# A delta-rule chain followed by a Fourier block: keys left unnormalised, weights rounded by integer instructions, and a chunk's outputs moved between the next step's products

## The chip, the core and the metric

One core of a Trainium2 chip runs the whole program. The metric is the device time of one execution in microseconds, from the runs listed below; a profiled execution is one more run of the same program, with its instructions recorded. The engines are TensorE (PE; its weight loads are listed apart as PEld), VectorE (DVE), ScalarE (ACT), GpSimd (POOL) and SyncE (SP, which here only issues transfers). Each takes its instructions strictly in the order in which they were built, and waits on semaphores for the others.

## The reference

There are two blocks. The first is a delta-rule recurrence for 4 batches, 8 heads, 768 steps and head dimension 48. With `k_n = k / (norm(k) + 1e-6)`, each step is

```
y[t]  = q[t] @ state
v_old = k_n[t] @ state
state = state + beta[t] * outer(k_n[t], v[t] - v_old)
```

The outputs, heads side by side (4 x 768 x 384), are the `x` of the second block: `u = x + real(fft(fft(x, axis=1), axis=2))`, then `u + relu(norm(u) @ w_ch1) @ w_ch2`, with `norm` the usual mean and variance over the last axis. `w_ch1` is 384 x 1536 and `w_ch2` 1536 x 384; both arrive as 64-bit floats, and the kernel turns them into 32-bit ones itself.

## The kernel before

The 768 steps of a batch are cut into 12 chunks of 64. Four chunks make a quad (12 quads over the batches), two quads a group (6 groups). For a group, `ahead` runs `prepare` on both quads and then `invert`:

- `prepare` squares the keys (`Ksq`, L302), sums them (L304), takes the root on POOL (`nrm`, L305), adds 1e-6 and inverts (L306, L307), and multiplies the keys by that (L308). TensorE then transposes keys and queries (`pt`, L127), ACT copies them to `KQT`, and the products `pg` of keys with keys and with queries go to `A` (ACT, L350) and `LQ` (DVE, L353).
- `invert` takes beta times the key products, 32 steps to a block, and solves for the inverse by 30 eliminations of two DVE instructions each (L379 and L381), for all blocks of the group at once. It ends with two DVE transposes (`Z`, L388, and L390) and four rounds of small products `pj`, copied by ACT into `wt`.

`chain(m)` then does one chunk: `pk = K state`, `R = V - pk` on DVE (L455), `pu = wt R`, copied by ACT to `U` (L464), `pS = K^T U`, added by DVE to the state (`st`, L475), and the outputs `py` = Q state + LQ U, copied by ACT to `x` (L488). The next chunk needs the new state, so the 48 chunks follow each other.

Beside the chain stand two generators. `pre` is `ahead` of the next group. `side` is, in batch 0, `weights`: 24 parts of 384 columns, in each of which ACT reads the two halves of the 64-bit numbers, POOL takes a maximum (L275), DVE cuts and shifts (L276, L277, L280) and POOL multiplies and adds (L282, L283). In later batches `side` is `second`: the Fourier products (`pf`, `pb`) and the two matrix products of the batch before (`ph` and `po`), with ReLU on ACT (L623). The last loop advances `pre` by 2.4 and `side` by 1.2 to 2.4 steps for each yield of the chain, and all of this is the order in which work is offered to a list scheduler; the scheduler then sets each engine's order with its own idea of durations. What an engine does next can therefore be seen only in the built order.

Sums in PSUM come from four pools: `pair` (2 tiles of two banks: `pg`, `pj`, `pk`, `pS`, `py`), `one` (2 of one bank: `pt`, `pu` and the two small start products) and `post` (2 of one bank, for everything of the second block).

Of the kernel before, what the change touches and what calls it, by code (L numbers as in the profile page):

```python
# [80 lines left out]
def kernel(  # L81
# [159 lines left out]
    def weights():  # L241
# [496 lines left out]
```

## Time and profile before

| | |
|---|---|
| runs | 927.81 us median of 3 (927.21 to 928.8) |
| profiled execution | 929.47 us, span of its instructions 927.8 us |
| mean granted TensorE clock | 0.847 of 2.4 GHz |
| busy: PE, DVE, ACT, POOL | 734.9, 411.7, 278.7, 176.2 us |
| last chunk's `U` (chunk 47) | starts at 772.41 us |
| after that | the second block of batch 3 alone |

How to read the rows further down: `A<-B` says that tile A is written from tile B. `x32` counts instructions. A row of the timeline begins with its start in us and its duration, and ends, in brackets, with the idle time of the engine just before it and what ended that. The granted clock says at which share of 2.4 GHz TensorE ran in a stretch; its other level is 1.2 GHz, 0.5 in the rows.

### The profile page before, as it was taken

Reading aid. Unit: us, or ns where it says so; the run is one execution under the profiler, and the core shown is the slowest. Engines: PE = TensorE matmul, PEld = TensorE weight load, DVE = VectorE, ACT = ScalarE, POOL = GpSimd, SP = SyncE. Lnnn points to the kernel's source line nnn. Section 1 sums busy time; section 2 is a strip of 40 time slices with the busy share of each in tenths; the row PEclk is TensorE's granted clock in tenths of the full one; section 3 lists DMA queues with packets and bytes.
Section 4 is the critical chain, followed back from the end, with each engine's and each line's share of the span. In section 5 each row is a group of like instructions: output and inputs, shape, how many; then the busy total and the mean of one; then the engine's idle time right before and its main releaser. Section 6 shows DMA issues by size and latency. Waiting matters only on the chain.

```text
span 927.8 us, 18288 instructions
## 1 busy us (share of the span) xinstructions
PE 734.9 (79%) x7768; PEld 548.2 (59%) x7768; DVE 411.7 (44%) x970; ACT 278.7 (30%) x649; POOL 176.2 (19%) x160
## 2 busy tenths in 40 slices
PE   1501686225797799988899998999999998999997
PEld 1401565124676667756667776677676766766774
DVE  4478426874468821187631583147821113500000
ACT  0513534235331531323612325243151212211210
POOL 6034634554501210000400004011100001100000
PEclk9755556556577879998799997999989998999999
DMA  7321134303110111210101110010000000000000
GB/s 148 65 82 68 24 97 103 92 1 91 35 18 10 23 23 29 41 42 4 21 17 41 22 43 2 10 27 1 26 11 10 9 10 10 1 17 9 9 18 17
DMA packets 84049, 30.77 MB, mean 33 GB/s; under 512 B 79488, under 2 KB 81216, under 8 KB 83584
## 3 DMA queue, kind: packets, MB, share of 16 engines
q1 hardware_dynamic: 77792, 25.18, 11.8%
q10 hardware_dynamic: 5408, 2.06, 0.9%
q0 software_dynamic: 768, 2.36, 0.7%
q8 instruction: 61, 1.00, 0.4%
q14 instruction: 20, 0.16, 0.1%
HBM read 24.87 MB, written 4.72 MB: 32 GB/s over the span
## 4 chain that ended last, share of the span: by engine, by line
PE 57%; DVE 18%; POOL 10%; ACT 6%; issue 4%; DMA 3%; SPq 2%; POOLq 0%; DVEq 0%; ACTq 0%
PE po L124 19%; PE ph L124 17%; PE py L124 6%; PE pu L124 3%; POOL nrm L305 3%; PE pf L124 3%; DVE X L381 2%; DVE sub L379 2%; PE pt L127 2%; POOL wtmp L275 2%; POOL wtmp L282 2%; PE pg L124 2%; POOL w L283 2%; SPq L153 2%; ACT A L350 1%
## 5 line engine op out<-in xcount | busy, mean ns | idle before, releaser
L124 PE MATMUL ph<-unT,w 128*128 128x256 f32 x864 | 220.5, 402 | 2.0 <-ACT hT L623 0.9
L124 PE MATMUL po<-w,hT 128*128 128x384 f32 x576 | 203.0, 500 | 0.0
L124 PEld LDWEIGHTS ph<-unT,w 128*128 128x128 f32 x864 | 162.7, 197 | 28.5 <-issue 2.5
L124 PEld LDWEIGHTS po<-w,hT 128*128 128x128 f32 x576 | 106.6, 192 | 65.6 <-issue 1.9
L623 ACT ACTIVATE hT<-ph 128x256 f32<-128x256 f32 x144 | 55.3, 384 | 189.3 <-PE ph L124 188.8
L503 POOL DMA_INDIRECT out_dram<-x,rows_hi x12 | 12.6, 1048 | 404.4 <-DVE x L636 246.2
L124 PE MATMUL pj<-Z,A 32*32 32x32 f32 x768 | 18.3, 212 | 79.8 <-DVE Z L388 79.8
L475 DVE TENSOR_TENSOR st<-st,pS 48x192 f32<-48x192 f32 x88 | 30.8, 350 | 89.6 <-PE pS L124 88.4
L381 DVE TENSOR_TENSOR X<-X,sub 128x30 f32<-128x30 f32 (+9 forms) x180 | 67.9, 377 | 4.3
L379 DVE TENSOR_TENSOR sub<-X 128x30 f32<-128x30 f32 (+9 forms) x180 | 66.3, 369 | 4.7
L636 DVE TENSOR_TENSOR x<-x,po 128x384 f32<-128x384 f32 x24 | 13.3, 552 | 118.2 <-PE po L124 118.2
L124 PEld LDWEIGHTS pj<-Z,A 32*32 32x32 f32 x768 | 16.9, 127 | 81.4 <-DVE Z L388 47.6
L455 DVE TENSOR_TENSOR R<-V,pk 128x192 f32<-128x192 f32 x48 | 16.9, 352 | 96.7 <-PE pk L124 96.3
L350 ACT ACTIVATE A<-pg 32x256 f32<-32x256 f32 x144 | 48.9, 370 | 23.5 <-PE pg L124 21.4
L124 PEld LDWEIGHTS pu<-R,wt 64*64 64x64 f32 x768 | 33.6, 163 | 32.4 <-DVE R L455 20.1
L124 PE MATMUL pu<-R,wt 64*64 64x48 f32 x768 | 40.4, 252 | 15.4 <-DVE R L455 15.3
L124 PE MATMUL py<-st,KQT 128*64 128x96 f32 x384 | 49.4, 280 | 3.3 <-DVE st L475 2.3
L464 ACT ACTIVATE U<-pu 128x192 f32<-128x192 f32 x48 | 15.9, 331 | 113.6 <-PE pu L124 113.4
L127 PE MATMUL pt<-pack,kp 128*128 128x128 f32 x96 | 24.5, 346 | 32.2 <-DVE nr L231 15.2
L488 ACT ACTIVATE x<-py 64x384 f32<-64x384 f32 x44 | 21.3, 484 | 81.9 <-PE py L124 81.7
L275 POOL TENSOR_SCALAR wtmp<-wtmp 128x384 f32<-128x384 f32 x24 | 29.4, 1225 | 84.4 <-ACT wtmp L274 84.4
L124 PEld LDWEIGHTS py<-st,KQT 128*64 128x64 f32 x384 | 39.1, 156 | 9.3 <-issue 2.2
(100 smaller groups left out, 956.9 us busy)
## 6 DMA issues: line engine op xcount, KB each, us to landing
w<-in_moe_w_ch_dram SPq DMA_DIRECT2D x6, 1536.0 KB, 6.6
V<-in_v_dram SPq DMA_DIRECT2D x96, 48.0 KB, 2.4
kp<-in_k_dram SPq DMA_DIRECT2D x96, 48.0 KB, 2.3
qp<-in_q_dram SPq DMA_DIRECT2D x80, 48.0 KB, 2.3
out_dram<-x SPq DMA_DIRECT2D x8, 192.0 KB, 1.9
qp<-in_q_dram ACTq DMA_DIRECT2D x16, 48.0 KB, 2.8
out_dram<-x SPq DMA_DIRECT2D x4, 168.0 KB, 2.1
stab<-k_stab ACTq DMA_DIRECT2D x1, 640.5 KB, 4.1
```

Source lines behind the costliest of these rows:

```text
L124: nc.tensor.matmul(o, lhsT=lhsT, rhs=rhs, start=start, stop=stop, skip_group_check=True)
L127: nc.tensor.matmul(o, lhsT=src, rhs=ident[0:src.shape[0], 0:src.shape[0]], is_transpose=True, start=start, stop=True, skip_group_check=True)
L153: eng.dma_start(out=dst[64 * hh:64 * hh + CH, c, :, 0:D], in_=src[b, 4 * hh:4 * hh + 4, t0:t0 + CH, :].rearrange("h p d -> p h d"))
L275: nc.gpsimd.tensor_scalar(a.bitcast(F32), a.bitcast(F32), FLOOR, None, op0=ALU.max)
L282: nc.gpsimd.tensor_tensor(low, low, pw.bitcast(F32), op=ALU.mult)
L305: nc.gpsimd.tensor_tensor(nrm, nrm, half_p, op=ALU.pow)
L350: nc.scalar.activation(ce(A[pr, ns, :, sl]), pv[pr, :, :, 0, c0:c0 + W], ACT.Copy)
L379: nc.vector.tensor_tensor(t, X[:, j:j + 1, j + 1:].broadcast_to([128, j, n]), X[:, 0:j, j:j + 1].broadcast_to([128, j, n]), op=ALU.mult)
L381: nc.vector.tensor_tensor(X[:, 0:j, j + 1:], X[:, 0:j, j + 1:], t, op=ALU.add)
L475: nc.vector.tensor_tensor(nst[pr, :, :, e, :], st[pr, :, :, e, :], pS[pr], op=ALU.add)
L488: nc.scalar.activation(xs[b][yr, T].rearrange("p (h u d) -> p h u d", h=2, u=4), py[yr], ACT.Copy, scale=live[yr] if n == NCH // 2 - 1 els ...
L623: nc.scalar.activation(hT[:, fc, :], ph, ACT.Relu)
```

## The change

Six things change together.

1. **Keys are not normalised.** The root, the reciprocal and the scaling of the keys leave `prepare`. `squares` lets ACT square the keys and DVE sum them; `norms_of(g)`, called once for a group after the elimination's first transpose, takes the root on ACT (Sqrt) with two refining steps on DVE, 12 instructions of at most 32 columns, and gives beta divided by the squared norm to the elimination. `scaled` multiplies a quad's V by the norms (one DVE instruction of 768 columns).
2. **Weights.** A part is now two ACT instructions and four DVE ones: a maximum, a bit operation, a shift, and `ADD32_U16LIMBS`, a custom instruction that adds 384 32-bit integers as 768 16-bit halves with carry. POOL has none. Transfers are of 768 KB instead of 1536 KB, into two alternating halves, and the next is issued when a half has been used.
3. **A chunk's outputs** (`py`) are no longer in `chain`: they are a generator that the next chunk advances, first behind its `pk`, then behind its `pu`.
4. **PSUM.** `pk`, `pu` and `pS` share one tile (`pc`, pool `ch`, one of two banks); `py` has one of its own; `pair` has 1 tile instead of 2; `post` is gone, and the second block shares the two tiles of `one` with `pt`.
5. **The start.** Only the unused columns of the key and query buffers are cleared. For the first two quads the key half of `prepare` comes first, with half of the copies to `A` on DVE; the query half runs beside the first elimination. Of the transfers that ACT issues, the queries of two quads now go ahead of the small tables.
6. **Pacing.** `side` is advanced by 1.0 instead of 1.2 a yield in batch 0, and starts before the first elimination. The second block of a batch starts after the first yield of the next batch's chunk.

The diff, cut to its core:

```diff
-    def ps_pair(name):
-        return ps.tile([128, 2, 512], F32, tag="pair", bufs=2, name=name)
+    def ps_pair(name, tag):
+        return ps.tile([128, 2, 512], F32, tag=tag, name=name)
...
-    def ps_post(shape, name):
-        return ps.tile(shape, F32, tag="post", bufs=2, name=name)
...
+    def scaled(Q):
+        if Q in vals and Q in lengths:
+            vf = vals[Q].rearrange("p c u d -> p (c u) d")
+            ln = lengths.pop(Q)
+            nc.vector.tensor_tensor(vf, vf, ln[:, :, None].broadcast_to([128, QT * 4, D]), op=ALU.mult)
...
-                nc.gpsimd.tensor_scalar(a.bitcast(F32), a.bitcast(F32), FLOOR, None, op0=ALU.max)
-                nc.vector.tensor_scalar(sg, hi, -2 ** 31, None, op0=ALU.bitwise_and)
-                nc.vector.scalar_tensor_tensor(a, a, 3, sg, op0=ALU.logical_shift_left,
-                                               op1=ALU.bitwise_or)
-                nc.vector.tensor_scalar(pw, a, -2 ** 23, None, op0=ALU.bitwise_and)
-                yield
-                nc.gpsimd.tensor_tensor(low, low, pw.bitcast(F32), op=ALU.mult)
-                nc.gpsimd.tensor_tensor(dst.rearrange("p c f -> p (c f)")[:, cs], low,
-                                        a.bitcast(F32), op=ALU.add)
+            nc.vector.tensor_scalar(mag.bitcast(F32), mag.bitcast(F32), FLOOR, None, op0=ALU.max)
+            nc.vector.scalar_tensor_tensor(low, hi, -2 ** 31, low, op0=ALU.bitwise_and,
+                                           op1=ALU.bitwise_or)
+            yield
+            nc.vector.tensor_scalar(mag, mag, 3, None, op0=ALU.logical_shift_left)
+            nc.vector._custom_dve(dve_ops.ADD32_U16LIMBS, out=dst.bitcast(u16),
+                                  in0=mag.bitcast(u16), in1=low.bitcast(u16))
+            if p % 2:
+                fetched(p // 2 + 2)
...
-        (nc.gpsimd if Q > 1 else nc.vector).tensor_tensor(Ksq, kf, kf, op=ALU.mult)
-        nc.vector.tensor_reduce(nrm, Ksq, axis=AX.X, op=ALU.add)
-        nc.gpsimd.tensor_tensor(nrm, nrm, half_p, op=ALU.pow)
-        nc.vector.tensor_scalar(nrm, nrm, 1e-6, None, op0=ALU.add)
-        nc.vector.reciprocal(nrm, nrm)
-        nc.vector.tensor_tensor(kf, kf, nrm[:, :, None].broadcast_to([128, nf, D]), op=ALU.mult)
+        nc.scalar.activation(Ksq, kf, ACT.Square)
+        nc.vector.tensor_reduce(ssq[g][:, lh], Ksq, axis=AX.X, op=ALU.add)
...
+    def norms_of(g):
+        nc.vector.tensor_scalar(x, x, 1e-30, None, op0=ALU.max)
+        nc.scalar.activation(lf, x, ACT.Sqrt)
+        for step in range(2):
+            nc.vector.reciprocal(t, lf)
+            nc.vector.tensor_tensor(t, t, x, op=ALU.mult)
+            nc.vector.tensor_tensor(lf, lf, t, op=ALU.add)
+            nc.vector.tensor_scalar(lf, lf, 0.5, 1e-6 * step, op0=ALU.mult, op1=ALU.add)
+        nc.vector.reciprocal(t, lf)
+        nc.vector.tensor_tensor(t, t, t, op=ALU.mult)
+        nc.vector.tensor_tensor(t, t, bcol[:, 2 * g:2 * g + 2].rearrange("p q n -> p (q n)"), op=ALU.mult)
+        nc.vector.transpose(bl, t)
...
-                pj = ps_pair("pj").rearrange("p h (c u t) -> p h c u t", c=QT, u=4)
+                pj = ps_pair("pj", "pair").rearrange("p h (c u t) -> p h c u t", c=QT, u=4)
...
-        yield
-        pu = ps_one([128, 4, D], "pu")
+        yield from advancing(later)
+        pu = pc[:, 0, 4 * D:8 * D].rearrange("p (u d) -> p u d", u=4)
...
+        later.append(outputs(b, n, c, KQT, LQ, st, U))
...
-    run(ahead(0))
+    for Q in (0, 1):
+        squares(Q)
+        run(prepare(Q, (0,)))
     values(0)
+    side = weights()
     tables()
-    side, pre = weights(), iter(())
+    run(both(invert(0), (x for Q in (0, 1) for x in prepare(Q, (1,)))))
+    scaled(0)
```

The built order shows two places. On TensorE, two chunks of quad 0 before (`st_82` and `st_84` are the two state buffers, `wt_76` and `kp_64` the inverse and the keys of quad 0):

```order
L124 MATMUL pk<-st_84,KQT 64x48 x8
L124 MATMUL pu<-R,wt_76 64x48 x8
L124 MATMUL pS<-U,kp_64 48x48 x8
L124 MATMUL py<-st_84,KQT 64x96 x4
L124 MATMUL py<-U,LQ 64x48 x8
L124 MATMUL pk<-st_82,KQT 64x48 x8
L124 MATMUL pu<-R,wt_76 64x48 x8
L124 MATMUL pS<-U,kp_64 48x48 x8
L124 MATMUL py<-st_82,KQT 64x96 x4
L124 MATMUL py<-U,LQ 64x48 x8
```

And the chunks of the same quad now (`pc` holds `pk`, `pu` and `pS` in turn):

```order
L123 MATMUL pc<-st_84,KQT 64x48 x8
L123 MATMUL py<-st_84,KQT 64x96 x4
L123 MATMUL pc<-R,wt_76 64x48 x8
L123 MATMUL pc<-U,kp_64 48x48 x8
L123 MATMUL py<-U,LQ 64x48 x8
L123 MATMUL pg<-KQT 64x128 x16
L123 MATMUL pc<-st_82,KQT 64x48 x8
L123 MATMUL py<-st_82,KQT 64x96 x4
L123 MATMUL pc<-R,wt_76 64x48 x8
L123 MATMUL pc<-U,kp_64 48x48 x8
L123 MATMUL py<-U,LQ 64x48 x8
```

The output product with the state has moved from behind `pS` to between `pk` and `pu`, and the one with `U` stands between `pS` and the next `pk`; some chunks also have `pg` of the next quad between them.

On DVE, the middle of the first elimination before (L379 and L381 are its two instructions; `wtmp` is a part of the weights):

```order
L276 TENSOR_SCALAR wtmp<-w_661 128x384
L379 TENSOR_TENSOR sub<-X 128x220
L381 TENSOR_TENSOR X<-X,sub 128x11x20
L379 TENSOR_TENSOR sub<-X 128x228
L277 SCALAR_TENSOR_TENSOR wtmp<-wtmp 128x384
L381 TENSOR_TENSOR X<-X,sub 128x12x19
L280 TENSOR_SCALAR wtmp<-wtmp 128x384
L379 TENSOR_TENSOR sub<-X 128x234
L381 TENSOR_TENSOR X<-X,sub 128x13x18
L379 TENSOR_TENSOR sub<-X 128x238
L276 TENSOR_SCALAR wtmp<-w_661 128x384
L381 TENSOR_TENSOR X<-X,sub 128x14x17
```

And now (L447 and L449 are the elimination; L304, L305, L308 and the ISA row L310 are the weights' four instructions):

```order
L447 TENSOR_TENSOR A<-X 128x12x19
L449 TENSOR_TENSOR X<-X,A 128x12x19
L305 SCALAR_TENSOR_TENSOR wtmp<-w_722,wtmp 128x384
L447 TENSOR_TENSOR A<-X 128x13x18
L304 TENSOR_SCALAR wtmp<-wtmp 128x384
L449 TENSOR_TENSOR X<-X,A 128x13x18
L308 TENSOR_SCALAR wtmp<-wtmp 128x384
L447 TENSOR_TENSOR A<-X 128x14x17
L310 ISA w_139<-wtmp 128x768
L449 TENSOR_TENSOR X<-X,A 128x14x17
L304 TENSOR_SCALAR wtmp<-wtmp 128x384
L447 TENSOR_TENSOR A<-X 128x15x16
```

Between two instructions of the elimination there is now one of the weights: 13 of the 24 parts stand inside the first elimination, where 4 were, and the last of the 24 stands before chunk 5. The second elimination begins behind that chunk, with no weights in it.

## Rows read from the trace of the kernel before

**Rows 1.** The page, part 1: busy time, share of span, instructions.

```profile
PE 734.9 (79%) x7768; PEld 548.2 (59%) x7768; DVE 411.7 (44%) x970; ACT 278.7 (30%) x649; POOL 176.2 (19%) x160
```

**Rows 2.** Stretches: from:to, length, busy by engine (count), TensorE clock, DMA share, GB/s.

```profile
43.00:86.00 43.00, 0.00 (x0) 0.00 (x0) 34.42 (x79) 4.95 (x10) 14.45 (x13) 0.50 0.28 87
166.00:200.00 34.00, 3.06 (x40) 2.59 (x40) 29.75 (x66) 5.57 (x12) 17.23 (x15) 0.50 0.22 61
...
310.00:335.00 25.00, 19.15 (x334) 14.36 (x331) 14.84 (x17) 12.78 (x23) 10.08 (x5) 0.63 0.05 10
335.00:416.00 81.00, 79.59 (x861) 55.39 (x859) 27.15 (x67) 24.61 (x63) 2.20 (x2) 0.99 0.17 36
416.00:435.00 19.00, 13.21 (x70) 11.54 (x71) 15.49 (x45) 3.96 (x9) 1.67 (x2) 0.82 0.06 10
435.00:460.00 25.00, 20.76 (x373) 16.23 (x372) 16.02 (x28) 15.76 (x33) 11.72 (x7) 0.80 0.07 12
...
550.00:573.00 23.00, 19.84 (x365) 15.42 (x364) 13.36 (x16) 13.12 (x25) 9.97 (x5) 0.77 0.06 12
```

**Rows 3.** Timeline of DVE: start, duration; first elimination's start, two ends.

```profile
45.01 0.19 DVE L379 TENSOR_TENSOR sub<-X 128x30 f32<-128x30 f32 x1
...
84.74 1.95 DVE L388 STREAM_TRANSPOSE Z<-Y 128x1024 f32<-128x1024 f32 x1
...
199.44 1.95 DVE L388 STREAM_TRANSPOSE Z<-Y 128x1024 f32<-128x1024 f32 x1
```

**Rows 4.** Timeline of ACT: `U` of chunks 0, 7, 8 and 11.

```profile
110.57 0.33 ACT L464 ACTIVATE U<-pu 128x192 f32<-128x192 f32 x1
...
165.91 0.33 ACT L464 ACTIVATE U<-pu 128x192 f32<-128x192 f32 x1 [1.39 <-PE pu L124]
...
220.85 0.33 ACT L464 ACTIVATE U<-pu 128x192 f32<-128x192 f32 x1 [4.24 <-PE pu L124]
...
247.19 0.33 ACT L464 ACTIVATE U<-pu 128x192 f32<-128x192 f32 x1 [1.06 <-PE pu L124]
```

**Rows 5.** Groups on DVE, 400 to 460 us: count, busy us, mean ns, idle.

```profile
L381 DVE TENSOR_TENSOR X<-X,sub 128x30 f32<-128x30 f32 (+14 forms) x30 | 11.0, 365 | 0.7
L379 DVE TENSOR_TENSOR sub<-X 128x30 f32<-128x30 f32 (+14 forms) x30 | 9.9, 330 | 0.7
```

**Rows 6.** Groups, whole span.

```profile
L623 ACT ACTIVATE hT<-ph 128x256 f32<-128x256 f32 x144 | 55.3, 384 | 189.3 <-PE ph L124 188.8
...
L305 POOL TENSOR_TENSOR nrm<-nrm,half_p 128x16 f32<-128x16 f32 x12 | 35.0, 2914 | 24.4 <-DVE nrm L304 22.4 <-DVE nr L230 2.0
...
L306 DVE TENSOR_SCALAR nrm<-nrm 128x16 f32<-128x16 f32 x12 | 14.7, 1225 | 31.6 <-POOL nrm L305 31.6
...
L277 DVE SCALAR_TENSOR_TENSOR wtmp<-wtmp 128x384 int32<-128x384 int32 x24 | 13.4, 557 | 22.5 <-POOL wtmp L275 22.4
...
L308 DVE TENSOR_TENSOR kp<-kp,nrm 128x768 f32<-128x768 f32 x12 | 11.5, 956 | 0.5
...
L280 DVE TENSOR_SCALAR wtmp<-wtmp 128x384 int32<-128x384 int32 x24 | 9.7, 404 | 0.4
```

**Rows 7.** Timeline, chunks 1 and 2: start, duration, instruction, idle before it.

```profile
121.69 1.54 PE L124 MATMUL py<-st,KQT 128*64 128x96 f32 x8
...
123.16 1.09 PE L124 MATMUL py<-U,LQ 64*64 64x48 f32 x16
...
124.84 0.68 PE L124 MATMUL pk<-st,KQT 48*64 48x48 f32 x16 [0.59 <-ACT x L488]
...
126.00 1.09 PE L124 MATMUL pu<-R,wt 64*64 64x48 f32 x16 [0.48 <-DVE R L455]
...
127.58 0.57 PE L124 MATMUL pS<-U,kp 64*48 64x48 f32 x16 [0.49 <-ACT U L464]
...
128.24 0.74 DVE L475 TENSOR_TENSOR st<-st,pS 48x192 f32<-48x192 f32 x2 [2.30 <-PE pS L124]
```

**Rows 8.** The chain that ended last, one piece: start, duration.

```profile
49.32 6.72 DMA w<-in_moe_w_ch_dram
```

More of the change, by code (lines that the diff above doesn't have):

```diff
@@ L182 @@
     nc.scalar.dma_start(out=bt[:, S // 2:S], in_=bflat[:, S // 2:S])
-    loads()
+    for Q in (0, 1):
+        fetch(Q, nc.sync, kps[Q], k)
+        fetch(Q, nc.scalar, qps[Q], q)
+        loaded[Q] = (kps[Q], qps[Q])
+    at["load"] = 2
     sel = const.tile([NBH, 2, NBH // 2], F32, name="sel")
@@ new lines, in weights, with fetched @@
+        nw = DFF // 2
+        halves = [(w1v[:, i, a * nw:a * nw + nw], w1[:, i, a * nw:a * nw + nw])
+                  for i in range(KD) for a in range(2)]
+        n2 = nw // DM
+        halves += [(w2v[:, i:i + n2], w2[:, i:i + n2]) for i in range(0, KF, n2)]
+        stage = wk.tile([128, 2, nw, 2], I32, tag="hT", name="w64")
+        def fetched(i):
+            if i < len(halves):
+                src, t = halves[i][0], stage[:, i % 2]
+                if len(src.shape) == 4:
+                    t = t.rearrange("p (c m) two -> p c m two", c=src.shape[1])
+                nc.sync.dma_start(out=t, in_=src)
@@ new lines, in weights, with words, first @@
+        np_ = nw // 2
+        tmps = [wk.tile([128, 2, np_], I32, tag=tag, name="wtmp") for tag in ("F", "scr")]
+        def words(p):
+            cs = slice(p % 2 * np_, (p % 2 + 1) * np_)
+            return stage[:, p // 2 % 2, cs, 0], stage[:, p // 2 % 2, cs, 1], tmps[p % 2]
+        def first(p):
+            lo, hi, t = words(p)
+            nc.scalar.activation(t[:, 0], lo.bitcast(mybir.dt.uint32), ACT.Copy, scale=2.0 ** -29)
+            nc.scalar.activation(t[:, 1].bitcast(F32), hi.bitcast(F32), ACT.Abs, scale=2.0 ** 16)
@@ new lines, in prepare @@
+    def prepare(Q, parts=(0, 1)):
+        i = quads[Q][1]
+        kp, qp = loaded[Q]
+        a0, na = parts[0], len(parts)
+        g, lh = divmod(Q, 2)
+        if 0 in parts:
+            if lh == 0:
+                grams[g] = wk.tile([128, 2 * QT, 4, 2, W], F32, tag="A", name="A")
+            KQT = wk.tile([128, QT, 2, 2, 2, CH], F32, tag="KQT", bufs=NB, name="KQT")
+            LQ = wk.tile([128, QT, 4, CH], F32, tag="LQ", bufs=NB, name="LQ")
+            held[Q] = (KQT, kp, LQ)
+        A = grams.get(g)
+        KQT, kp, LQ = held[Q]
@@ L343, in ce @@
                 return t.rearrange("p c (j e) t -> p e (c j) t", e=2)
-            for hh in range(2):
+            for hh in range(2 if 0 in parts else 0):
                 for r in range(2):
@@ L417, in invert @@
                 yield
+    later = []
     def chain(m):
@@ L424, in chain @@
         if c == 0:
-            held.pop(Q - 1, None)
-            at["chain"] = Q
-            loads()
-            if Q + 1 < len(quads):
-                values(Q + 1)
+            scaled(Q)
         V4 = vals[Q]
@@ L461, in chain @@
                 pr = slice(64 * hh, 64 * hh + 64)
-                mm(pu[pr, u], wt[pr, c, u], R[pr, u], u == 0)
-        U = wk.tile([128, 4, D], F32, tag="U", name="U")
+                mm(pu[pr, u], wt[pr, c, u], R[pr, u], True)
+        U = wk.tile([128, 4, D], F32, tag="U", bufs=2, name="U")
         nc.scalar.activation(U, pu, ACT.Copy)
-        yield
-        if not last:
-            pS = ps_pair("pS")[:, :, 0:2 * D].rearrange("p h (j d) -> p h j d", j=2)
+        yield from advancing(later)
+        if c == 0:
+            held.pop(Q - 1, None)
+            at["chain"] = Q
+            loads()
+            if Q + 1 < len(quads):
+                values(Q + 1)
+        if n < NCH - 1:
+            pS = pc[:, :, 2 * D:4 * D].rearrange("p h (j d) -> p h j d", j=2)
             for j in range(2):
@@ L489, in chain, with advancing @@
                              scale=live[yr] if n == NCH // 2 - 1 else 1.0)
+    def advancing(gens):
+        if gens and next(gens[0], "end") == "end":
+            gens.pop(0)
         yield
@@ L689 @@
         b, n = divmod(m, NCH)
-        if n == 0 and b > 0:
-            run(side)
-            side = second(b - 1)
         if m % (2 * QT) == 0:
@@ L697 @@
             due = [0.0, 0.0]
-        for _ in chain(m):
+        for i, _ in enumerate(chain(m)):
+            if n == 0 and b > 0 and i == 1:
+                run(side)
+                side = second(b - 1)
             due[0] += PRE
@@ L705 @@
                         advance(gen)
+    for gen in later:
+        run(gen)
     run(side)
```

168 lines of the change are left out of this document (90 added, 78 removed).

## The prediction

> **What bounds the kernel now.** I read the busy times first: TensorE is busy 79% of the span and no other engine more than 44% [rows 1]. That is an average over two different kernels, so the table of stretches comes next [rows 2]. From 335 to 416 us TensorE is busy 79.6 of 81 us at a granted clock of 0.99: it is the bound there, and moving work between other engines gains nothing. From 43 to 86 us it does nothing at all, from 166 to 200 us 3 us, and DVE is busy 34.4 and 29.8 us: these are the first two eliminations. Between full stretches lie four short ones (310 to 335, 416 to 435, 435 to 460, 550 to 573 us) in which TensorE has gaps and its clock stands between its two levels, at 0.63 to 0.82. Then the timeline of `U` gives the pace of the chain: chunk 0 at 110.6 us, chunk 7 at 165.9, chunk 8 only at 220.9, chunk 11 at 247.2 [rows 4]. The eliminations explain this: the first runs from 45.0 us to the transpose of its result at 84.7, the second ends at 199.4 [rows 3], and chunk 8 needs the second. So about 250 us of the span wait on DVE and on hand-overs between engines, and what follows is TensorE's work. What is gained before chunk 11 should pass to the end in full, since the work behind it is the same.
>
> **The change, step by step, as times of the new kernel.**
>
> *Start.* Two roots of 2.9 us on POOL, two additions of 1.2 and two scalings of 0.96 [rows 6] leave the path to the first transpose: up to 10.2 us. On it come squares and a Sqrt with one more table load on ACT, and the start's small tables now stand behind sixteen query loads in ACT's queue, so that the selector needed by TensorE's first products comes later. Between 0 and 10.2 I take 2.5: the elimination starts at 42.5 us instead of 45.0.
>
> *First elimination.* It held 4 parts of the weights and now holds 13. Undisturbed it takes 11.0 + 9.9 = 20.9 us [rows 5]. A part costs DVE two one-source instructions (0.404 each, as the shift of before), one bit operation (0.557) and the carry-add. No row has a custom instruction or 16-bit elements. Its bounds are the nearest rows: 0.404 for one source of 384 columns below, 0.956 for two sources of 768 columns above [rows 6]. I take 0.557, the two-source row on the same 384 words, so a part is 1.92 us. The Trainium skill ("VectorE: DVE Perf Modes", section "The perf-mode tier table (the rule you actually need)") says that two 16-bit tensors in SBUF pass two results a cycle only where a program for that mode exists, and one otherwise; by the first my sum stands, by the second 0.956 is right and the first rival below comes out. No run shows yet which.
> 13 parts are 25.0 us. Add some 3 us of small work that stands between (one V scaling of 0.96 and a handful like the state's 0.37 each), 1.2 for the last product, and 2.5 for one wait on a weight transfer: 1.5 MB took 6.7 us [rows 8], half as much is now under way at a time, but the third half is queued on SP behind 24 query and value loads. The sum is 20.9 + 25.0 + 3 + 1.2 + 2.5 = 52.6, so `Z` comes at 95.1 us, 10.4 later than before. The step alone is a loss; it pays because POOL is out of the conversion and the weights end about chunk 5 instead of chunk 11.
>
> *From `Z` to `U` of chunk 0.* Before it took 25.8 us (84.7 to 110.6), and 21.4 in group 1 (199.4 to 220.9). In both, the keys of the next two quads are normalised in between: 2 x (2.9 + 1.2 + 0.96) = 10.1 us, in front of state and residual on DVE. Gone, 25.8 becomes 15.7; I take 14, since the POOL products go too, but not less, because `pj` has one PSUM tile and its four rounds now follow each other strictly. `U` of chunk 0: 109 us, against 110.6.
>
> *Chunks 0 to 7.* Before, 7 steps in 55.3 us, 7.9 each. In the timeline of one step [rows 7] `pk` starts at 124.84 and the new state is there at 128.98, 4.1 us later, but the next `pk` had to wait for both `py` (1.54 and 1.09 us) and for the PSUM tile that the copy of `py` frees. Now the 1.54 stands where TensorE idled 0.48 for the residual (it adds 1.0), the 1.09 where it would wait 0.8 for the state (it adds 0.3): 5.5 us. Seven are 38.5; 2 more for weights in front of state or residual in DVE's order: 40.5. `U` of chunk 7: 149.5, against 165.9.
>
> *Second elimination.* It now stands behind chunk 5's state: 109 + 5 x 5.8 = 138, plus 2 to the state, plus 3.2 for the transpose and the product with beta: 143. Undisturbed 20.9, seven state and residual instructions 2.5, a V scaling 1.0, the last product 1.2, some 2 of waiting for TensorE in between: `Z` at 171. Then 21.4 - 10.1 = 11 us: `U` of chunk 8 at 182, against 220.9. Here most of the gain is made.
>
> *Chunks 8 to 11.* Before 26.3 us for three steps; now 5.5 and 1 for the next quads' products: 19.5. `U` of chunk 11 at 201.5, against 247.2: **45.7 us**.
>
> *Later.* TensorE's work is unchanged. Of the four hand-over stretches, counted as length less busy time times clock, 12.9 + 8.2 + 8.4 + 7.7 = 37 us are not work at full clock [rows 2]. About 10 of the 21 us from `Z` to `U` go with the normalising, but `pj` gets slower and TensorE fills part of it with other products already. I take a third, **12 us**, between 0 and 25; the Fourier block's own waits stay.
>
> The sum: 929.47 (profiled, span 927.8) - 45.7 - 12 = 871.8. The profiled execution lies 1.7 above the median of 927.81, so the median should be about **870 us**.
>
> **The rivals.**
>
> *The carry-add passes one 16-bit half a cycle* (0.956). 24 x 0.4 = 9.6 us more on DVE, 5.2 in the first elimination and the rest before chunk 5, nearly all on the path: **879 us**. For it: the row of 768 two-source columns. The skill's rule above is this rival.
>
> *The hand-overs vanish whole*: 25 instead of 12, and a start nearer to its 10 us: **850 us**. For it: the normalising is the longest piece in all four.
>
> *Later stretches lose to shared PSUM a little*, or a weight transfer holds the in-order DVE in the first elimination longer: 15 to 30 us back, **892 us**.
>
> *Slower than before.* One mechanism: `ph`, `po`, `pf` and the transposes `pt` share two PSUM tiles where each side had two. A `po` holds one for its 12 products; if the other alone is left, each `ph` group must wait for the copy of the one before, 0.384 us and about as much in signals, 0.7 together. Of the 144 groups [rows 6] all but the last batch's 36 run while `pt` exists: 108 x 0.7 = 76 us, **946 us**. It decides from 58 / 0.7 = 83 groups on. Against it: the built order puts `pt` beside few of the groups, and chain products, which use other tiles, fill the wait.
>
> *No change*: the interleaving is in the built order, so only a loss that happens to equal the gain would do this.
>
> **How the numbers follow.** My forecast has 0.53, with its own range 857 to 884; the carry-add at one a cycle 0.20; hand-overs whole 0.12; the mild loss 0.10; slower 0.04; no change 0.01. The range 846 to 902 leaves out the slower case, and the ends of two others. Three runs of this kernel spread by 0.17%, so a change under 0.2% can't be told from none: faster 0.94, same 0.02, slower 0.04.
>
> **What would show it.** Right: `Z` of group 0 later than 84.7 but `U` of chunk 0 near 109; steps of 5.5 to 6 us in quads 0 and 1; no POOL instruction in the weights, the last part near chunk 5; `U` of chunk 8 near 182 and chunk 11 near 201; the carry-add at 0.5 to 0.6 us; stretches like 310 to 335 with a higher clock. Wrong: gaps of TensorE that end with the copy of `ph` or `pt`; a chunk 8 that still waits until 200, for instance because the third weight half lands late; or a second half that grows by what the first gave.

## The result, and the profile after

The changed kernel took **857.73 us** (median of 4 runs, 854.05 to 862.04) against 928.30 for the kernel before (4 runs, 927.21 to 929.32): ratio **0.9242**, 95% interval 0.9196 to 0.9288, 70.6 us less. The forecast was 870 (846 to 902). The profiled execution took 858.76 us, with a span of 857.1 and a mean granted clock of 0.896, against 929.47, 927.8 and 0.847. A run more than 1.5% above the fastest of its kernel is left out of the medians below; that is one run of `again`, at 865.92 us.

| place | before | predicted | after |
|---|---|---|---|
| first elimination starts | 45.0 | 42.5 | 41.5 |
| `Z` of group 0 | 84.7 | 95.1 | 81.4 |
| `U` of chunk 0 | 110.6 | 109 | 95.2 |
| `U` of chunk 7 | 165.9 | 149.5 | 136.0 |
| `Z` of group 1 | 199.4 | 171 | 158.0 |
| `U` of chunk 8 | 220.9 | 182 | 171.6 |
| `U` of chunk 11 | 247.2 | 201.5 | 191.5 |
| end (profiled) | 929.5 | 871.8 | 858.8 |

The page's first part after, which answers to [rows 1]; POOL has gone from 176.2 us to 42.7, and TensorE is about as busy (734.9 us before):

```profile
PE 727.7 (85%) x7896; PEld 541.3 (63%) x7896; DVE 404.9 (47%) x1060; ACT 284.6 (33%) x662; POOL 42.7 (5%) x63
```

Stretches after, columns as in [rows 2]: the first elimination, from `Z` to `U` of chunk 0, the second elimination, chunks 8 to 11, a later hand-over (from `Z` of group 3 to the next chunk's `U`), and what follows it:

```profile
41.50:81.40 39.90, 9.85 (x84) 7.46 (x80) 38.04 (x121) 14.92 (x35) 0.00 (x0) 0.67 0.57 153
81.40:95.20 13.80, 7.21 (x208) 6.55 (x208) 9.57 (x16) 11.88 (x21) 0.00 (x0) 0.50 0.24 70
136.00:158.00 22.00, 6.37 (x68) 4.33 (x67) 18.52 (x51) 2.56 (x7) 0.00 (x0) 0.50 0.17 30
...
171.50:191.50 20.00, 18.61 (x344) 16.95 (x344) 8.05 (x25) 7.76 (x23) 1.26 (x1) 0.50 0.12 21
...
367.00:380.00 13.00, 10.86 (x236) 8.91 (x237) 8.86 (x17) 11.22 (x23) 0.94 (x2) 0.96 0.10 18
380.00:401.00 21.00, 19.09 (x268) 14.89 (x266) 12.43 (x41) 8.90 (x24) 2.23 (x3) 0.78 0.06 11
```

DVE is still what the two eliminations wait for (busy 38.0 of 39.9 and 18.5 of 22 us). From `Z` to `U` the busiest engine is now ACT (11.9 of 13.8). From 171.5 to 191.5 TensorE itself is the bound (18.6 of 20), at the lower clock.

DVE's timeline after, for [rows 3]: the first elimination's start, and the end of the first two.

```profile
41.47 0.18 DVE L447 TENSOR_TENSOR A<-X 128x30 f32<-128x30 f32 x1
...
81.41 2.02 DVE L456 STREAM_TRANSPOSE Z<-Y 128x1024 f32<-128x1024 f32 x1
...
157.95 2.02 DVE L456 STREAM_TRANSPOSE Z<-Y 128x1024 f32<-128x1024 f32 x1
```

`Z` of group 0 comes 3.3 us earlier than before, where 10.4 later was forecast. The first elimination itself takes 39.9 us with 13 parts of the weights, against 39.7 before with 4; it starts 3.5 us earlier. ACT's timeline after, `U` of chunks 0, 7, 8 and 11, for [rows 4]:

```profile
95.22 0.33 ACT L530 ACTIVATE U<-pc 128x192 f32<-128x192 f32 x1
...
135.95 0.33 ACT L530 ACTIVATE U<-pc 128x192 f32<-128x192 f32 x1 [0.49 <-PE pc L123]
...
171.57 0.33 ACT L530 ACTIVATE U<-pc 128x192 f32<-128x192 f32 x1
...
191.47 0.33 ACT L530 ACTIVATE U<-pc 128x192 f32<-128x192 f32 x1 [2.71 <-PE pc L123]
```

Each is 10 to 15 us earlier than forecast, and the distances between them are near the forecast's.

Groups after, for [rows 6]: the weights' bit operation and the carry-add.

```profile
L305 DVE SCALAR_TENSOR_TENSOR wtmp<-w,wtmp 128x384 int32<-128x384 int32 x24 | 13.3, 553 | 2.1 <-ACT wtmp L288 2.0
...
L310 DVE CUSTOM_DVE_ANT_0 w<-wtmp 128x768 uint16<-128x768 uint16 x24 | 13.2, 551 | 0.1
```

The carry-add took 0.551 us for 768 halves, as long as the bit operation for 384 words (0.553), and about the 0.557 that the sum used. The Trainium skill ("VectorE: DVE Perf Modes", section "The perf-mode tier table (the rule you actually need)") lets two 16-bit tensors pass two results a cycle where a program for that mode exists. The trace agrees, and the rival with 0.956 is out.

One step of the chain after, for [rows 7]:

```profile
116.80 0.48 PE L123 MATMUL pc<-st,KQT 48*64 48x48 f32 x15
...
117.21 0.88 PE L123 MATMUL py<-st,KQT 128*64 128x96 f32 x8
...
117.53 0.35 DVE L521 TENSOR_TENSOR R<-V,pc 128x192 f32<-128x192 f32 x1
...
118.01 0.37 PEld L123 LDWEIGHTS pc<-R,wt 64*64 64x64 f32 x10
```

The output product (`py`) runs while DVE makes the residual, and the weights of the product with `R` are loaded from 118.01, 0.13 us after the residual's end: the output product holds nothing up here.

The one term that is far off is the first elimination: 39.9 us where 52.6 were summed. DVE's timeline in the middle of it, with three of the four instructions of a part of the weights (L305, L308 and L310) each between two of the elimination (L447 and L449), and the same two of the elimination alone in the second one:

```profile
60.09 0.40 DVE L447 TENSOR_TENSOR A<-X 128x240 f32<-128x240 f32 x1
60.41 0.55 DVE L305 SCALAR_TENSOR_TENSOR wtmp<-w,wtmp 128x384 int32<-128x384 int32 x1
60.88 0.40 DVE L449 TENSOR_TENSOR X<-X,A 128x240 f32<-128x240 f32 x1
61.20 0.35 DVE L308 TENSOR_SCALAR wtmp<-wtmp 128x384 int32<-128x384 int32 x1
61.47 0.40 DVE L447 TENSOR_TENSOR A<-X 128x240 f32<-128x240 f32 x1
61.79 0.55 DVE L310 CUSTOM_DVE_ANT_0 w<-wtmp 128x768 uint16<-128x768 uint16 x1
...
143.68 0.41 DVE L447 TENSOR_TENSOR A<-X 128x240 f32<-128x240 f32 x1
144.12 0.41 DVE L449 TENSOR_TENSOR X<-X,A 128x240 f32<-128x240 f32 x1
```

Alone, the two start 0.44 us apart with records of 0.41: each needs the result of the one ahead. With an instruction of the weights between them, which needs neither, they start 0.79 us apart (60.09 to 60.88) or 0.59 (60.88 to 61.47): the one between begins 0.08 us before the record ahead of it ends, and so does the next. So an instruction in such a gap adds 0.79 - 0.44 = 0.35 us and not its 0.55, or 0.15 and not 0.35. A part of four would be 2 x 0.35 + 2 x 0.15 = 1.0 us, not 1.92.

### The profile page after: what moved, and what is told of

Its sections match the earlier page's. It is cut to its first block, busy times and chain, and to the rows that moved or that the text cites. A ratio compares the mean times of both kernels' runs of the same rounds, so it can differ in the third digit from the quotient of the medians.

```text
span 857.1 us, 18540 instructions
## 1 busy us (share of the span) xinstructions
PE 727.7 (85%) x7896; PEld 541.3 (63%) x7896; DVE 404.9 (47%) x1060; ACT 284.6 (33%) x662; POOL 42.7 (5%) x63
## 4 chain that ended last, share of the span: by engine, by line
PE 65%; DVE 15%; ACT 9%; DMA 4%; SPq 3%; issue 3%; POOL 1%; POOLq 0%; ACTq 0%; DVEq 0%
PE ph L123 21%; PE po L123 20%; PE py L123 7%; PE pc L123 6%; PE pg L123 3%; SPq L155 3%; PE pf L123 2%; DVE X L449 2%; DVE A L447 2%; DMA kp<-in_k_dram 2%; PE pj L123 2%; PE pb L123 2%; ACT A L392 1%; ACT wt L484 1%; DVE Z L456 1%
## 5 line engine op out<-in xcount | busy, mean ns | idle before, releaser
L547 DVE TENSOR_TENSOR st<-st,pc 48x192 f32<-48x192 f32 x88 | 30.8, 350 | 104.3 <-PE pc L123 65.5
L449 DVE TENSOR_TENSOR X<-X,A 128x30 f32<-128x30 f32 (+9 forms) x180 | 60.3, 335 | 4.2
L447 DVE TENSOR_TENSOR A<-X 128x30 f32<-128x30 f32 (+9 forms) x180 | 59.3, 329 | 4.1
L530 ACT ACTIVATE U<-pc 128x192 f32<-128x192 f32 x48 | 15.9, 330 | 114.9 <-PE pc L123 109.9
L123 PEld LDWEIGHTS pj<-Z,A 32*32 32x32 f32 x768 | 16.5, 126 | 57.4 <-DVE Z L456 53.4
L123 PE MATMUL pc<-R,wt 64*64 64x48 f32 x768 | 40.6, 244 | 12.9 <-DVE R L521 7.2
L123 PEld LDWEIGHTS pc<-R,wt 64*64 64x64 f32 x768 | 32.8, 154 | 28.7 <-issue 9.9
L123 PE MATMUL pg<-KQT 48*64 48x128 f32 (+1 forms) x896 | 38.7, 316 | 6.7 <-ACT KQT L359 5.4
L123 PE MATMUL py<-U,LQ 64*64 64x48 f32 x768 | 41.5, 242 | 0.0
L123 PEld LDWEIGHTS pg<-KQT 48*64 48x64 f32 x896 | 30.2, 173 | 14.0 <-ACT KQT L359 9.0
L123 PEld LDWEIGHTS py<-U,LQ 64*64 64x64 f32 x768 | 34.9, 155 | 3.5 <-issue 2.3
```

Source lines behind the costliest of these rows:

```text
L123: nc.tensor.matmul(o, lhsT=lhsT, rhs=rhs, start=start, stop=stop, skip_group_check=True)
L447: nc.vector.tensor_tensor(t, X[:, j:j + 1, j + 1:].broadcast_to([128, j, n]), X[:, 0:j, j:j + 1].broadcast_to([128, j, n]), op=ALU.mult)
L449: nc.vector.tensor_tensor(X[:, 0:j, j + 1:], X[:, 0:j, j + 1:], t, op=ALU.add)
L530: nc.scalar.activation(U, pu, ACT.Copy)
L547: nc.vector.tensor_tensor(nst[pr, :, :, e, :], st[pr, :, :, e, :], pS[pr], op=ALU.add)
```

## The experiments

Times are medians with the range, and the ratio to runs of the kernel before on the same chip with its 95% interval. *After* is the changed kernel. Places such as `U` of a chunk are read from one profiled execution of each run.

| run | us | range | ratio | interval |
|---|---|---|---|---|
| `hold` | 859.03 | 855.85 to 864.51 | 0.9273 | 0.9236 to 0.9309 |
| `u_weights` | 890.82 | 885.82 to 890.87 | 0.9578 | 0.9544 to 0.9612 |
| `u_outputs` | 863.71 | 856.79 to 866.46 | 0.9298 | 0.9241 to 0.9354 |
| `u_norms` | 902.93 | 892.33 to 904.56 | 0.9728 | 0.9704 to 0.9752 |
| `u_psum` | 880.80 | 877.11 to 883.53 | 0.9494 | 0.9445 to 0.9544 |
| `early` | 856.71 | 853.18 to 859.92 | 0.9236 | 0.9182 to 0.9291 |
| `warm` | 862.26 | 853.40 to 864.04 | 0.9255 | 0.9185 to 0.9325 |
| `again` | 859.79 | 852.17 to 861.63 | 0.9258 | 0.9222 to 0.9294 |
| `early2` | 850.79 | 846.26 to 856.67 | 0.9188 | 0.9158 to 0.9219 |
| `best` | 834.71 | 830.70 to 840.65 | 0.9011 | 0.8979 to 0.9043 |

`micro` is not the kernel: it ran once, 181.65 us.

### `hold`: no weights in the first elimination

```diff
+        for i in range(2):     # kept[0] is Z of group 0
+            nc.vector.tensor_copy(stage[:, i, 0:1, 0], kept[0][:, 0, 0, 0:1].bitcast(I32))
...
+        kept.append(Z)
```

> Leaves nothing of the result out: the weights' first two transfers are made to wait for Z of group 0, so no part of the weights lies in the first elimination. Theory 1 (a part that is put between dependent steps costs DVE about 1.0 us, since independent instructions start before the one ahead has ended): the first elimination, 39.9 us with 13 parts, becomes 39.9 - 13 x 1.0 = 27 us, Z at about 68 to 69 us. Rival (a part costs its full 1.7 us as its four durations say, and something else in the stretch was cheaper than predicted): 39.9 - 13 x 1.7 = 18 us, Z at 59 to 60 us. The whole time: the weights move to chunks 0 to 15 and the second elimination; 857 with 850 to 868.

DVE's timeline in `hold`, the elimination's first instruction and `Z`:

```profile
40.87 0.65 DVE L451 TENSOR_TENSOR A<-X 128x30 f32<-128x30 f32 x1
...
68.17 2.02 DVE L461 STREAM_TRANSPOSE Z<-Y 128x1024 f32<-128x1024 f32 x1
```

27.3 us instead of 39.9: the 13 parts cost 12.6 us, **0.97 each**. The theory stands, the rival (`Z` at 59) falls. Chunk 0 came 13.4 us earlier, chunk 8 4.2 later (175.8), chunk 12 at 194.3 as in *after* (194.2), and the whole is the same. The parts cost as much elsewhere: chunks 0 to 7 took 46.5 us instead of 40.7, and from there to chunk 8 it was 47.5 instead of 35.6. Chunks 8 to 11 then took 16.5 instead of 19.9, with the same 344 products at a granted clock of 0.76 instead of 0.50.

### `micro`: DVE alone

```python
for _ in range(24):      # stretch (5) in short; (4) has a shift, (6) a carry-add in place of bits
    pair_mult(t, X); bits(aa); pair_add(X, t); bits(aa)
```

> DVE alone, none of the reference's work. Seven stretches of 24 rounds each, on 128x384 words and on the elimination's pair of 128x12x19: (1) a shift, each on the result of the last; (2) two such chains in turn; (3) the pair alone; (4) the pair with a shift in each of its two gaps; (5) the pair with a bit operation in each gap; (6) the pair with a carry-add in each gap; (7) the carry-add, each on the last. Theory (an instruction that doesn't need the one ahead starts before that one's record ends): us a round (1) 0.44, (2) 0.60 for two, (3) 0.88, (4) 1.18, (5) 1.58, (6) 1.58, (7) 0.59. Rival (one at a time, each for its whole duration): (2) 0.88, (4) 1.7, (5) 2.0, (6) 2.0.

DVE's timeline in `micro`: first instruction of stretches (3), (4) and (5), and the instruction that follows the last of each:

```profile
30.79 0.40 DVE L73 TENSOR_TENSOR t<-X 128x228 f32<-128x228 f32 x1
...
51.39 0.16 DVE L47 TENSOR_TENSOR join<-join,X 128x1 f32<-128x1 f32 x1
...
53.45 0.35 DVE L81 TENSOR_SCALAR aa<-aa 128x384 int32<-128x384 int32 x1
...
81.05 0.15 DVE L46 TENSOR_TENSOR join<-aa,bb 128x1 f32<-128x1 f32 x1
...
83.30 0.56 DVE L89 SCALAR_TENSOR_TENSOR aa<-dd,aa 128x384 int32<-128x384 int32 x1
83.77 0.39 DVE L87 TENSOR_TENSOR t<-X 128x228 f32<-128x228 f32 x1
84.08 0.56 DVE L91 SCALAR_TENSOR_TENSOR aa<-dd,aa 128x384 int32<-128x384 int32 x1
...
120.49 0.17 DVE L46 TENSOR_TENSOR join<-aa,bb 128x1 f32<-128x1 f32 x1
```

A round of (3) takes 20.60 / 24 = 0.86 us, of (4) 1.15, of (5) 1.55; in the same way (1) 0.39, (2) 0.54 for two shifts, (6) 1.55, (7) 0.59. A shift in a gap costs (1.15 - 0.86) / 2 = **0.15 us**, a bit operation or carry-add **0.35**; the rival's 1.7 and 2.0 a round are far off. All seven are at or a little below the theory's numbers. The Trainium skill ("Vector Engine (DVE) Microarchitecture Reference", section "5.2 Measured stream behaviour on trn2 (trn3 not measured)") gives 1.04 ns a column and some 75 ns an instruction once the queue overlaps; an estimate from that is 0.475 us for 384 columns and 0.31 for 228. The trace agrees: where neither instruction needs the other, the next one starts 0.47 us after one of 384 columns (83.30 to 83.77) and 0.31 after one of 228 (83.77 to 84.08).

### `u_weights`: the weights as before

```diff
-            nc.vector._custom_dve(dve_ops.ADD32_U16LIMBS, out=dst.bitcast(u16),
...
+                nc.gpsimd.tensor_tensor(low, low, pw.bitcast(F32), op=ALU.mult)
+                nc.gpsimd.tensor_tensor(dst.rearrange("p c f -> p (c f)")[:, cs], low,
+                                        a.bitcast(F32), op=ALU.add)
```

> The weights as before (1.5 MB at a time, roots of the rounding on POOL, four parts a piece), all else as changed. By the prediction's accounting the second elimination again waits on POOL: U of chunk 0 earlier than 95 (about 90), U of chunk 8 some 20 to 30 us later than 171.6, and the whole 15 to 35 us slower than 857.7. Rival (the weights hardly count, the norms and the interleaving carry the gain): within 8 us of 857.7.

Groups on POOL in `u_weights`:

```profile
L285 POOL TENSOR_SCALAR wtmp<-wtmp 128x384 f32<-128x384 f32 x24 | 28.6, 1192 | 75.8 <-ACT wtmp L284 75.8
L292 POOL TENSOR_TENSOR wtmp<-wtmp 128x384 f32<-128x384 f32 x24 | 25.9, 1078 | 42.0 <-DVE wtmp L290 38.4 <-DVE ssq L392 3.6
```

33 us slower than *after*, as expected. `U` of chunk 8 at 199.8 is 28.2 later, as expected too. Chunk 0 at 97.8 is later and not earlier, where 90 was expected: the first elimination took 43.2 us with the old parts and 39.9 with the new, so it loses nothing by them. The weights carry nearly half of the gain: 28.2 us at chunk 8, 33.4 at chunk 11, and no more behind that.

### `u_outputs` and `u_psum`: the outputs, and PSUM

```diff
-        later.append(outputs(b, n, c, KQT, LQ, st, U))
+        run(outputs(b, n, c, KQT, LQ, st, U))
```

> The outputs of a chunk run right behind its state again, all else as changed. By the prediction's accounting a step of chunks 0 to 7 goes from 5.8 to some 7.2 us: U of chunk 7 and of chunk 11 are 10 to 14 us later, and the whole 8 to 15 us slower. Rival (TensorE's order is set by what is ready, the interleaving changes nothing): U of chunk 7 within 3 us of 135.95 and the whole within 3 us.

6 us slower, with ranges that overlap; `U` of chunk 7 at 138.1 (2.2 later), a step 6.09 us instead of 5.82. The accounting fails here: the place in the code gives 0.3 us a step of the 1.4 expected. In `u_outputs` the product with the state still runs between `pk` and the product with `R` (`pk` at 112.35, `py` at 112.96, `R` at 114.43). `u_psum` adds the old tiles:

```diff
-        return ps.tile([128, 2, 512], F32, tag=tag, name=name)
+        return ps.tile([128, 2, 512], F32, tag="pair", bufs=2, name=name)
...
-        pu = pc[:, 0, 4 * D:8 * D].rearrange("p (u d) -> p u d", u=4)
+        pu = ps_one([128, 4, D], "pu")
```

> As u_outputs (outputs right behind the state), and PSUM shared out as before: pk, pS, py, pg and pj take turns on two tiles, pu on the two of pt, the second block has two of its own. Theory: it is the shared tiles and not the place in the code that put both output products in front of the next pk, so only now do the steps of chunks 0 to 7 grow from 6.1 to 7 or more: U of chunk 7 at 145 or later (138.1 in u_outputs), the whole 8 to 20 us above u_outputs' 863.7. Rival (neither matters; the short steps come from the weights' place on DVE alone): U of chunk 7 within 3 us of 138.1, the whole within 4 us of 863.7.

Timeline of `u_psum` around one step:

```profile
121.34 0.73 DVE L548 TENSOR_TENSOR st<-st,pS 48x192 f32<-48x192 f32 x2 [0.23 <-PE pS L126]
...
121.99 0.67 PE L126 MATMUL py<-U,LQ 64*64 64x48 f32 x16
...
123.24 0.45 PE L126 MATMUL pk<-st,KQT 48*64 48x48 f32 x16 [0.58 <-ACT x L568]
```

The state is there at 122.07; `pk` starts at 123.24, when the copy of `py` has freed its tile. `U` of chunk 7 at 147.5, a step 7.04 us, the whole 17 us above `u_outputs`. With the outputs behind the state, the tiles are worth 0.95 us a step; what they are worth with the outputs in their new place was not run. From 7.04 to the 7.9 of before another 0.9 us a step are left, which neither edit explains.

### `u_norms`: the keys normalised as before

```diff
-        nc.scalar.activation(Ksq, kf, ACT.Square)
+        (nc.gpsimd if Q > 1 else nc.vector).tensor_tensor(Ksq, kf, kf, op=ALU.mult)
...
+        nc.gpsimd.tensor_tensor(nrm, nrm, half_q, op=ALU.pow)
```

> The keys are normalised as before (square, root on POOL, reciprocal, scaling of the keys before their transposes), all else as changed. By the prediction's accounting the start is 2.5 us later, and Z to U of chunks 0 and 8 takes some 10 us more each, the later hand-overs some 3 us each: 15 to 35 us slower than 857.7. Rival (the chain no longer waits for the keys, other work stands there anyway): Z to U unchanged at 13.6 to 13.8 us, the whole within 8 us.

45 us slower, more than either theory said (the profiled execution, at 892.33, is the lowest of five). The start went the other way: the elimination began at 38.9, 2.5 us earlier than in *after*, where 2.5 later was expected. From `Z` to `U` of chunks 0 and 8 took 21.1 and 17.7 us (13.8 and 13.6 in *after*): 7.2 and 4.1 of the 10. But chunk 11 is only 7.2 us later than in *after*, chunk 47 34.9: most is lost behind. Stretches of `u_norms` behind `Z` of group 3:

```profile
384.00:404.00 20.00, 10.72 (x218) 8.82 (x219) 11.61 (x11) 9.38 (x17) 9.99 (x5) 0.50 0.04 7
404.00:425.00 21.00, 20.90 (x264) 17.15 (x263) 5.10 (x16) 9.73 (x25) 0.93 (x2) 0.82 0.12 21
```

While POOL takes its roots, TensorE is busy 10.7 of 20 us at 0.50. In *after* the like stretch, 367 to 380, has 10.86 of 13 at 0.96. So the old norms cost this hand-over twice, in idle time and in clock. The stretch behind it has no lower clock than in *after* (0.82 against 0.78 from 380 to 401), but more work: chunk 26 came 37.1 us after chunk 24 with 397 products between, in *after* 27.4 us after it with 322.

### `early` and `early2`: the start

```diff
-    for Q in (0, 1):
-        fetch(Q, nc.sync, kps[Q], k)
-        fetch(Q, nc.scalar, qps[Q], q)
...
+    for eng, Q in ((nc.sync, 0), (nc.scalar, 1)):
+        fetch(Q, eng, kps[Q], k)
+        fetch(Q, eng, qps[Q], q)
```

> Nothing is left out; only the start's transfers change: ACT issues its small tables first, then keys and queries of quad 1, SP keys and queries of quad 0. The selector, issued at 14.1 us now, is issued at about 3, the keys of quad 1 by 9 instead of 12.2. Theory: the path to chunk 8 is bound by DVE and latency from the first transpose on, so the elimination starts at 33 to 35 instead of 41.5, U of chunk 8 comes 7 us earlier (about 164.5), and the whole is about 851 (848 to 854). Rival (as in hold, where chunk 0 came 13.4 us earlier and chunk 12 not at all, the lead is lost before chunk 12): 855 to 860.

The two fetches now stand behind the small tables. The first transpose came at 7.6 us instead of 19.3, but the elimination's `X` at 35.1 as in *after* (35.2), and the whole is the same: the lead never arose. ACT's timeline in `early`:

```profile
11.87 5.72 ACTq L155 DMA_DIRECT2D qp<-in_q_dram  x8
17.62 1.28 ACT L329 ACT_TABLE_LOAD   x1 [17.62 <-DMA V<-in_v_dram]
18.92 0.84 ACT L329 ACTIVATE Ksq<-kp 128x768 f32<-128x768 f32 x1
```

ACT issues transfers until 17.6 (these 8 at 0.72 us each) and computes nothing before. `U` of chunk 8 came at 171.7 as in *after*, of chunk 11 at 187.8, 3.7 earlier: between them the same 344 products ran at 0.78 and not at 0.50. `early2` takes the queries off ACT:

```diff
+        fetch(Q, nc.sync, kps[Q], k)
...
+        fetch(Q, nc.gpsimd, qps[Q], q)
```

> Nothing is left out. In early TensorE's first transposes came at 7.6 us and not 19.3, but ACT stood behind its 25 transfer issues until 17.6 and squared the first keys at 18.9, as late as in the changed kernel. Here ACT issues its nine small transfers alone, SP the keys of both quads, POOL the queries. Theory (ACT's issues bound the start): ACT is free at about 7, the first squares stand at 9 to 10, the second quad's transposes at 15, the first elimination starts at 31 to 33 instead of 41.5, U of chunk 8 at 161 to 164 instead of 171.6, and the whole is 7 to 10 us below the changed kernel's. Rival (the lead is lost before chunk 12, as in hold): less than 3 us below.

Squares at 13.0, elimination at 34.3 (7.1 earlier), `U` of chunk 8 at 166.6 (5.0 earlier), the whole 9.0 us below `again`: that ACT's issues bound the start stands, with single times 1 to 5 us later than expected, since ACT now waits until 11.7 for the first keys to land. Not all of the 9.0 is shown to be the start's: of the 8.9 us by which chunk 11 was earlier than in *after*, 3.9 came between chunks 8 and 11 with a clock of 0.78, as in `early`, which had no lead.

### `warm`: products that nobody reads

```diff
+            if warm is not None and j >= 6:
+                mm(warm[0:W, j % 2], bt, stab[:, 0:512], True)
```

> Nothing is left out; 24 products of 512 columns whose result nobody reads are added on TensorE in the second elimination, where it was busy 6.4 of 22 us. Theory: the granted clock stays above 0.5 up to chunk 8, where it was 0.50 from 136 to 191 us; Z to U of chunk 8 goes from 13.6 to about 10 us, the 18.6 busy us of 171.5 to 191.5 become some 10, and U of chunk 11 comes 8 to 12 us earlier; of that, between 3 and 10 us reach the end: 848 to 855. Rival (chunk 12 waits for DVE, since it came at 194.2 in the changed kernel and in hold alike): U of chunk 12 within 2 us of 194.2 and the whole within 3 us of 857.7.

Stretches of `warm`:

```profile
128.00:158.00 30.00, 29.08 (x218) 10.78 (x216) 26.88 (x72) 3.09 (x8) 0.00 (x0) 1.00 0.18 32
...
162.00:172.00 10.00, 8.93 (x164) 7.84 (x166) 1.62 (x3) 9.77 (x19) 0.00 (x0) 0.50 0.13 23
172.00:192.00 20.00, 18.83 (x343) 16.77 (x344) 9.01 (x27) 8.42 (x22) 1.27 (x1) 0.50 0.11 18
```

The clock was 1.00 while these products ran, and 0.50 from 162 on, where TensorE was busy 8.9 of 10 and 18.8 of 20 us with the kernel's own small products. Between the two, from 158 to 162, it was busy 1.3 of 4 us; whether that gap or the smaller products took the clock down was not separated. Chunk 8 came at 170.8 instead of 171.6 and chunk 11 at 192.7 instead of 191.5: the theory falls. Chunk 12 at 195.4 is within the rival's 2 us; the whole, 862.26, is 4.5 above 857.7 where it said 3, with ranges that overlap.

### `again` and `best`

> The changed kernel itself, beside the two below on one chip: 854 to 862 us, as in its first four runs.

It did: 859.79, ratio 0.9258. The next run is `best`:

```diff
-                        nc.scalar.activation(wt[r1, :, :, 0:W], Z[r1, ns], ACT.Copy)
+                        nc.gpsimd.tensor_copy(wt[r1, :, :, 0:W], Z[r1, ns])
```

> early2, and the four copies per quad of Z into wt (0.63 us each on ACT) go to POOL. In the changed kernel, from Z to U of chunk 0, ACT is busy 11.9 of 13.8 us, and a copy of Z stands ahead of each copy out of pj. Theory: Z to U of chunks 0 and 8 goes from 13.7 to 11 or 12 us, each later hand-over gains up to 2 us, and the whole is 3 to 8 us below early2. Rival (TensorE's order, with the second quad's pj ahead of the first chunk's products, or a slower copy on POOL takes it back): Z to U within 1 us of 13.7, the whole within 3 us of early2.

16 us below `early2`, where 3 to 8 were expected, and 25 below `again`, both outside the intervals. The reason given holds in part only. From `Z` to `U` of chunk 0 it gained nothing (13.9 us, where 11 to 12 were expected): parts of the weights took the copies' place on ACT, and a `pj` still stands inside chunk 0's products. For chunk 8 it gained 1.4. Up to chunk 24 `best` was no earlier than `early2` (369.6 against 369.4). Of the 15.3 us at chunk 47, 5.9 arose from chunk 24 to 26 and 7.8 from `Z` of group 5 to chunk 42. Stretches in `early2`: chunks 8 to 11, behind `U` of chunk 24, the hand-over behind `Z` of group 5, and what follows it:

```profile
166.50:182.60 16.10, 14.05 (x344) 12.42 (x344) 8.05 (x25) 7.73 (x22) 1.27 (x1) 0.78 0.12 22
...
370.00:397.00 27.00, 24.50 (x321) 18.56 (x321) 15.12 (x50) 9.73 (x25) 3.15 (x5) 0.85 0.05 9
595.00:608.00 13.00, 9.69 (x227) 8.04 (x225) 4.31 (x3) 9.31 (x18) 0.00 (x0) 0.83 0.00 1
608.00:645.00 37.00, 37.00 (x360) 25.31 (x359) 4.69 (x12) 7.62 (x18) 0.00 (x0) 0.88 0.02 7
```

And the same in `best`:

```profile
162.60:182.60 20.00, 18.62 (x344) 16.97 (x344) 5.48 (x14) 7.62 (x21) 1.26 (x1) 0.50 0.12 22
...
370.00:391.00 21.00, 19.92 (x319) 15.71 (x320) 13.35 (x45) 8.42 (x23) 3.15 (x5) 1.00 0.06 12
588.00:599.00 11.00, 10.59 (x237) 8.15 (x237) 3.86 (x3) 5.39 (x11) 4.84 (x8) 1.00 0.01 3
599.00:645.00 46.00, 46.00 (x489) 33.12 (x489) 6.91 (x18) 10.04 (x24) 1.00 (x1) 1.00 0.03 10
```

The stretch of chunks 24 to 26 is 6 us shorter. Behind both hand-overs, which are now fuller (10.59 of 11 us busy against 9.69 of 13; for group 3, 10.83 of 12 against 11.73 of 14), the clock is 1.00 and not 0.85 or 0.88. But behind `Z` of group 1, where the hand-over is 1.4 us shorter too, it is the other way: the same 344 products ran at 0.50 in `best` and at 0.78 in `early2`. So a fuller hand-over went with a higher clock behind it in two places and with a lower one in a third, in one profiled execution each. What sets the clock there is not shown.

## Why the prediction was right, and which term was off

- **What bounds it** and the order of the gains: right. 55.7 of 70.7 us were there at chunk 11, and passed to the end whole.
- **The number**: 857.7 lies in the range of 846 to 902, at the lower edge of the forecast's own 857 to 884 and nearer to the 850 of the rival "the hand-overs vanish whole" than to 870. That it is not this rival is read from the places: of the 13.0 us by which the end came earlier than forecast, 10.0 were there at chunk 11, ahead of the later hand-overs.
- **Start**: 2.5 taken, 3.5 measured, but not by the mechanism. The prediction let the gain come from the norms; with the old norms (`u_norms`) the elimination starts 2.5 us earlier still. What bounds the start is the transfers in ACT's queue (`early`, `early2`), which the prediction named only for the selector.
- **First elimination**: the failed term. "13 parts are 25.0 us" took four records a part, one after the other; `hold` and `micro` show 0.97 to 1.0 us a part, 12.6 in all. This one term is 12.4 of the 13.0 us between 871.8 and 858.8. With it falls "the step alone is a loss": it took 39.9 us against 39.7 before. The 2.5 us of waiting for a weight transfer did not come either: DVE's one wait there was 1.7 us for `pc`. Without parts 27.6 were summed and 27.3 measured (`hold`): the rest held only as a whole.
- **`Z` to `U` of chunk 0**: 14 taken, 13.8 measured, in part by luck. The prediction gave 10.1 of the gain to the norms; `u_norms` gives them 7.2 here and 4.1 at chunk 8, so 4.8 and 3.7 us come from the rest of the change. A piece of the 10.1 was no price of the norms: the addition of 1.2 us took 0.17 in `u_norms` when POOL was idle (13.80) and 1.44 beside POOL's squares (394.31). Why the rest is not less (the one tile of `pj`) was not tested alone; ACT, busy 11.9 of 13.8, is a rival, and taking its copies off it gained nothing here (`best`).
- **Chunks 0 to 7**: 40.5 taken, 40.7 measured. The mechanism was half right: of the 2.1 us a step, the tiles are the larger piece (0.95), the place of the product in the code the smaller (0.3), and 0.9 stays open.
- **Second elimination and chunk 8**: 32.5 from chunk 7 taken, 35.6 measured: from `Z` to `U` took 13.6 and not 11.
- **Chunks 8 to 11**: 19.5 taken, 19.9 measured.
- **Later**: 12 taken, 15.0 measured. These 3.0 us too little and the 3.1 us too much that were expected to be gained up to chunk 8 cancel, which is luck. `u_norms` shows that the old norms cost some 28 us behind chunk 11, the lower clock in a hand-over included.
- **Rivals**: none came true. The carry-add took 0.551; the later stretches gained 15 and not 25, and gave nothing back; the shared tiles of `ph` cost nothing to speak of: before `ph` TensorE waited 5.0 us in all. The last part of the weights stood in front of chunk 4.

Undone one at a time, weights (33), norms (45) and outputs with tiles (23) give 101 us, more than the 71 of all. They don't add up; a likely reason, not tested, is that each undone part makes the chain wait where the others would have gained. The new start and the pacing were not undone alone.

## What to carry to other kernels

Price an instruction that goes between two dependent ones by distances from start to start in the trace, not by its record: here 0.47 + 0.31 - 0.43 = 0.35 us for one with a record of 0.55. Before moving transfers to a compute engine's queue, count its issues as that engine's work. Where TensorE's clock is not full behind a hand-over, look at the gaps in it first, and measure: filling them went with the full clock behind two hand-overs of `best`, not behind a third.

## What the runs showed of the hardware

- DVE starts an instruction 0.08 us before the record ahead ends if it does not need it, and 0.03 after if it does (`micro`: 0.31 and 0.43 us from start to start, with records of 0.39 and 0.40).
- A DVE instruction can last as long as POOL's beside it: an addition of 128x16 ran from 394.31 to 395.75 beside squares on POOL from 394.26 to 395.72, and took 0.17 us with POOL idle (`u_norms`). No run isolates this.
- A busy TensorE is not a fast one: 18.8 busy us of 20 at 0.50 (`warm`). What in its work made the difference was not separated.
- The first four runs of the changed kernel spread by 0.9%, those of the kernel before by 0.2%, but beside `early` the latter spread by 0.9% too (924.70 to 932.93), so the prediction's "under 0.2%" is too fine. The mean clock does not order the times: 856.70 us came at 0.908 and 854.05 at 0.903, and the kernel before took 925.98 at 0.850 and 925.99 at 0.904. The cause stays open.
